# Last two attention chunks routed as one group, the last mixing ahead of routing products, and the last weight pieces behind the last exponential

## The chip, the cores and the metric

The kernel runs on 1 core of one Trainium2 chip. The metric is the device time of one execution in microseconds (us). The engines are named as in the profile: PE (TensorE matmuls), PEld (its weight loads), DVE (VectorE), ACT (ScalarE), POOL (GpSimd) and SP (SyncE, which here issues plain DMAs). Each engine works through its own instructions in the order in which the program issues them, and waits where an input or a buffer of another engine is not ready.

## The reference

Three stages follow each other on 1536 tokens of width 384 (2 batches, 768 steps, 8 heads of 48).

```python
# gated linear attention
for t in range(S):
    state = alpha[:, :, t, :, None] * state + k[:, :, t] (x) v[:, :, t]
    y[:, :, t] = q[:, :, t] @ state
# first layer of experts: each token goes to its best of 8 experts
logits = x @ w_gate;  expert = argmax(logits);  gate = softmax(logits)[expert]
out = gate * (relu(x @ w1[expert]) @ w2[expert])          # up to a capacity per expert
# second layer: noisy gate, two best experts per token
noisy = x @ w_gate + log1p(exp(x @ w_noise)) * noise
out = sum over the top two of softmax weight * (relu(x @ w1[e]) @ w2[e])
```

## The kernel before, in words

**Attention.** The 1536 tokens are 12 chunks of 128. For each chunk `scores` (L298) makes the transposed keys and the masked key-query products, `state` (L322) carries the state on, `mix` (L348) makes the mixed values (copied out of PSUM by ACT, L365), and `logits` runs `r1_logits` (L379): eight matmuls L385 give the token rows and their gate products in one PSUM tile. DVE sums the gate products (`gates`, L387), ACT copies the rows (L394). For chunks 8 to 11 ("late" chunks) ACT also copies a rounded row into a `late` tile (L399), and POOL writes the remainder beside it (L400).

**Routing.** `GROUPS` says which chunks are routed together. `r1_group` (L371) makes the row tile of a group when its first chunk has its logits. `route1` (L404) is a generator; each `R` runs one of its eight steps: maximum; index of the maximum and difference (L417, L418); one-hot (L420); exponential (ACT, L422); rank products on PE (L426 to L430); sums and slots (L432 to L435); for late chunks the one-hot of the slot (L442), the row index (L445) and the running count (L447); and the scatter of each chunk's rows into `xs1` by an indirect DMA that POOL issues (L158, with a small memset L156 ahead of it).

**The written order.** `PATTERNS` holds a string for each chunk index `i`, which the main loop reads letter by letter: S scores of the next chunk, T state, L logits of chunk `i-1`, M mixing of `i`, R one routing step, D a decay step, W one weight piece. `FXR` holds the same for what stands behind the loop: l logits of the last chunk, R a routing step, x a step of `first_x`. All engines get their instructions in this program order.

**The first expert's tokens.** `first_x` (L650) gathers them without a trip through memory for the late chunks: three steps with the rows that were loaded early (`early`, four matmuls L655 each), one step for each of the late chunks 8 to 11 (six matmuls L662 each, which need the late row, its remainder and its slot one-hot), and a last step that copies the result as a high and a low part (L669 on ACT, L670 on DVE).

**Weight pieces.** `split` (L525) cuts a weight tile in 16 pieces; for each ACT makes the rounded high part (L537), and the low part, a subtraction (L538) on DVE or POOL, is put on the list `rest`. `split_rest` issues what is on the list. `splits(k)` in the main loop first calls `split_rest` and then makes piece `k`. The last letters of `WE` give the pieces 13, 14 and 15 to POOL and piece 12 to DVE. Pieces 8 to 15 belong to the second product of the first expert, 12 to 15 to its blocks 4 to 7.

**Behind the gather.** `split_rest()` (L1148) issues what is left, then a few constants are made, among them `lates`: an iota on POOL (L1030) and its conversion on ACT (L1032). Then the experts begin: `hidden` (L675) makes a block of 128 hidden units for the first expert's tokens, nine matmuls (L683, L686), a relu on ACT (L692) and a remainder on DVE (L693). Its PSUM tiles have the tag `ph`, with three buffers.

Of the kernel before, what the change touches and what calls it, by code (L numbers as in the profile page):

```python
# [35 lines left out]
IW = HR + E  # L36
PIECES = [(0, 0, 2), (0, 2, 2), (0, 4, 2), (1, 0, 3), (1, 3, 3)]
PARTS = [[(0, 0, 1), (0, 1, 1)]] + [[a] for a in PIECES[1:]]
GROUPS = [(0, 3), (3, 3), (6, 2), (8, 2), (10, 1), (11, 1)]
MASKS = "G" * 12  # L40
STATES = "AAAAAAAAVVVV"
DECAYS = "444444440000"
# [1 line left out]
S0 = 1  # L44
WARM1 = 2
WARM2 = 10
FXR = "xRRxRRlxRRRRRxxRxRR"
EARLY = 8
WE = "GGGGVVVVVVVVVGGG"
PATTERNS = (  # L50
    "SDDTDDM", "SDDTLDDM", "SDDTLDDM", "SDDTLRRRDDM", "SDDTLDDM", "SRRDTLRRRDDDM",
    "SDDTLRRRDDM", "WSDDTWLDDMW", "WSRRWTRRRWLRRRWMW", "RWSRWTRRRWLWMW", "STLRRRWWMW", "RRRRRLRRRM")
LATE = (0, 4)
LZ = 0
LR = (5, 6, 7, 5, 7, 8)
# [12 lines left out]
def body(tc, ap, cap, dbg=False, stop=False):  # L68
    nc = tc.nc
    V, A, G, PE = nc.vector, nc.scalar, nc.gpsimd, nc.tensor  # L70
    with ExitStack() as ctx:
# [5 lines left out]
        def sb(shape, tag, bufs, dt=F32):  # L77
            cnt[0] += 1
            return pool.tile(list(shape), dt, name=f"{tag}_{cnt[0]}", tag=tag, bufs=bufs)
# [4 lines left out]
        def s6(shape, dt=F32):  # L84
            return sb(shape, "s6", 18, dt)
# [20 lines left out]
        def pm():  # L106
            return ps("pm", 2)
# [44 lines left out]
        NCK = B * NC  # L152
# [218 lines left out]
        def r1_group(js):  # L371

            n = len(js)
            row, l = s6([128, n, RW]), sm([128, 3, E], "l")[:, :n]
            G.tensor_copy(row[:, :, TK:], nt[:, js[0]:js[0] + n, :])
            for k, j in enumerate(js):
                grp[j] = (js, row, l, k)

        def r1_logits(j, first=True):  # L379
            js, row, l, k = grp[j]  # L380
            yT = yTs.pop(j)
            lg = pm()
            lv = lg[:, :4 * IW].rearrange("p (g n) -> p g n", g=4)
            for gp in range(4):
                PE.matmul(lv[:, gp, :], yT[:, gp, :], idw[:, gp, :], start=True, stop=True)  # L385
            def gates():
                V.tensor_reduce(l[:, k, :], lv[:, :, HR:].rearrange("p g n -> p n g"), axis=AX.X, op=ALU.add)  # L387


            if j == NCK - 1:  # L390
                gates()
            by = lambda x: x.rearrange("p (g a e) -> p g a e", g=4, a=2)
            for ab in range(2):
                A.activation(by(row[:, k, :DM])[:, :, ab, :], lv[:, :, ab * 64:ab * 64 + 48], AF.Copy)  # L394
            if j < NCK - 1:
                gates()
            if j >= EARLY and first:
                t = late[j] = sb([128, 2 * DM + C1], "b6", 5, F32R)
                A.activation(t[:, :DM], row[:, k, :DM], AF.Copy)  # L399
                G.tensor_tensor(t[:, DM:2 * DM], row[:, k, :DM], t[:, :DM].bitcast(F32), op=ALU.subtract)  # L400
            if dbg:
                nc.sync.dma_start(ap["xdbg"][j * 128:(j + 1) * 128], row[:, k, :DM])
# [122 lines left out]
        def split(n, q, eng=None):  # L525

            if n >= len(jobs):
                return
            i, h = divmod(q, 4)
            t = raws[n, i]  # L530
            if h == 0:
                shp = [128, ND, 512] if i < 2 else [128, 4, DM]
                parts[n, i] = (s6(shp, F32R), s6(shp, F32R))
            hi, lo = parts[n, i]
            sl = (slice(None), slice(None), slice(h * 128, h * 128 + 128)) if i < 2 else (
                slice(None), slice(h, h + 1), slice(None))
            A.activation(hi[sl], t[sl], AF.Copy)  # L537
            rest.append(lambda: (eng or V).tensor_tensor(lo[sl], t[sl], hi[sl].bitcast(F32), op=ALU.subtract))  # L538
# [111 lines left out]
        def first_x():  # L650

            at = [py()[:, :C1] for _ in range(ND)]
            for d in range(ND):
                for t in range(T1):
                    PE.matmul(at[d][:, t * P1:(t + 1) * P1], early[0][:, t, d * 128:(d + 1) * 128], ident[:P1, :P1],  # L655
                              start=(t == 0), stop=False, skip_group_check=True)
                yield
            n = N // 128
            for j in range(EARLY, n):
                for d in range(ND):  # L660
                    for i in range(2):
                        PE.matmul(at[d], late[j][:, i * DM + d * 128:i * DM + (d + 1) * 128], late[j][:, 2 * DM:],  # L662
                                  start=False, stop=(i == 1 and j == n - 1), skip_group_check=True)
                yield
            xg[0] = sb([P1, T1, RW], "b6", 5)
            nc.sync.dma_start(xg[0][:, :, DM:], xs1[:C1, DM:].rearrange("(t p) d -> p t d", p=P1))
            xh, xl = xsp[0] = (xb([128, ND, C1], F32R), xb([128, ND, C1], F32R))
            for d in range(ND):
                A.activation(xh[:, d, :], at[d], AF.Copy)  # L669
                V.tensor_tensor(xl[:, d, :], at[d], xh[:, d, :].bitcast(F32), op=ALU.subtract)  # L670
            yield
# [396 lines left out]

        groups = [tuple(range(g, g + n)) for g, n in GROUPS]
        routes, extra = [], []  # L1070

        def logits(j):
            for g in groups:
                if g[0] == j:
                    r1_group(g)
            r1_logits(j)
            for g in groups:
                if g[-1] == j:
                    routes.append(route1(g))

        def route_on():
            if routes and next(routes[0], 0) == 0:
                routes.pop(0)
# [19 lines left out]
        si, wi = S0, 0  # L1103
# [28 lines left out]
        fx = first_x()  # L1132
        for o in FXR:
            if o == "x":
                next(fx)
            elif o == "l":
                logits(NCK - 1)
            else:
                route_on()
        while routes:  # L1140
# [404 lines left out]
```

## Time and profile before

| | |
|---|---|
| median of 3 runs | 457.68 us (457.44 to 457.8) |
| profiled execution | 457.59 us, its span 456.0 us |
| PE busy | 445.1 us (98%) |
| POOL busy | 347.6 us (76%) |
| DVE, ACT busy | 273.0 us (60%), 266.3 us (58%) |
| DMA | 93.66 MB, mean 205 GB/s |

The profile is one execution, recorded by the hardware. Busy time is the share of the span in which an engine had an instruction running; PE's ends are modelled, so its starts are the firmer numbers. A releaser ("<-") names what ended an engine's idle time. In a timeline, `x6` says that six instructions of one line follow each other and the time is from the start of the first to the end of the last. The end of attention, where the change lies, is at 77 to 94 us of the span.

### The profile page before, as it was taken

The page shows a single profiled execution, that of the slowest core. Times are in us where ns is not written, and L with a number is a line of the kernel's source. Part 1 is how long each engine was busy: PE and PEld are TensorE (multiplying, and loading weights), DVE is VectorE, ACT ScalarE, POOL GpSimd, SP SyncE. Part 2 cuts the span into 40 slices and gives each one's busy share as a digit, 9 for nine tenths or more (in the row PEclk, how much of TensorE's full clock was granted, in tenths as well). Part 3 has the DMA queues.
Part 4 walks back from the last instruction along what each step waited for, and adds up shares of the span by engine and source line. Part 5 has one row for each costly group of instructions (what it writes and reads, how often), then busy time and mean ns, then how long its engine had stood idle before and what let it go on. Part 6 is the DMA issues. An engine that isn't in the chain of part 4 may idle for free.

```text
span 456.0 us, 9516 instructions
## 1 busy us (share of the span) xinstructions
PE 445.1 (98%) x3167; PEld 418.4 (92%) x3170; DVE 273.0 (60%) x906; ACT 266.3 (58%) x703; POOL 347.6 (76%) x436
## 2 busy tenths in 40 slices
PE   8999999999999999999999999999999999999992
PEld 3688888899999999999999999999999999999992
DVE  8989986856967867878866454333443343243350
ACT  3577787467776776786651468255473464664310
POOL 3434697785998989999943379989989698799922
PEclk9999999999999999999999999999999999999997
DMA  8974972869999987876321997649287492993232
GB/s 284 407 269 150 327 260 96 259 199 313 329 307 314 269 253 224 269 226 193 123 70 55 253 324 229 136 108 323 57 262 154 129 293 57 284 246 51 27 45 43
DMA packets 73586, 93.66 MB, mean 205 GB/s; under 512 B 31962, under 2 KB 56610, under 8 KB 73526
## 3 DMA queue, kind: packets, MB, share of 16 engines
q1 hardware_dynamic: 66854, 79.98, 57.4%
q0 software_dynamic: 6672, 12.97, 12.7%
q8 instruction: 27, 0.44, 0.4%
q14 instruction: 33, 0.27, 0.2%
HBM read 70.30 MB, written 20.02 MB: 198 GB/s over the span
## 4 chain that ended last, share of the span: by engine, by line
PE 95%; DMA 1%; ACT 1%; POOL 0%; DVE 0%; issue 0%; POOLq 0%; ACTq 0%
PE ph L683 24%; PE py L722 22%; PE ph L686 12%; PE py L714 8%; PE py L716 4%; PE ph L170 4%; PE ph L309 3%; PE pm L750 3%; PE pm L385 2%; PE py L336 2%; PE py L362 2%; PE py L356 2%; DMA s<-w 1%; PE py L303 1%; PE ph L1002 1%; PE ph L975 1%
## 5 line engine op out<-in xcount | busy, mean ns | idle before, releaser
L538 POOL TENSOR_TENSOR s<-s,s 128x384 fp32r<-128x384 f32 x211 | 221.1, 1169 | 17.9 <-ACT s L537 16.3
L683 PE MATMUL ph<-x,s 128*128 128x240 f32 (+9 forms) x768 | 133.1, 308 | 0.3 <-DVE h L693 0.2
L537 ACT ACTIVATE s<-s 128x384 fp32r<-128x384 f32 x256 | 124.9, 517 | 9.5 <-DMA s<-w 7.6
L683 PEld LDWEIGHTS ph<-x,s 128*128 128x128 f32 x768 | 116.2, 189 | 1.9 <-DVE h L693 0.4
L693 DVE SCALAR_TENSOR_TENSOR h<-ph,h 128x240 fp32r<-128x240 f32 (+9 forms) x128 | 60.2, 470 | 82.8 <-ACT h L692 80.7
L692 ACT ACTIVATE h<-ph 128x240 fp32r<-128x240 f32 (+9 forms) x128 | 54.1, 423 | 75.7 <-PE ph L686 70.6
L686 PE MATMUL ph<-x,s 128*128 128x240 f32 (+9 forms) x384 | 76.2, 306 | 0.0
L158 POOL DMA_INDIRECT out<-b,m_ix x28 | 44.0, 1571 | 29.4 <-ACT b L878 9.7
L722 PE MATMUL py<-h,s 128*128 128x304 f32 (+4 forms) x360 | 65.4, 339 | 0.0
L722 PEld LDWEIGHTS py<-h,s 128*128 128x128 f32 x360 | 63.2, 188 | 0.8
L714 PE MATMUL py<-h,s 128*128 128x480 f32 (+3 forms) x192 | 61.5, 376 | 0.0
L686 PEld LDWEIGHTS ph<-x,s 128*128 128x128 f32 x384 | 60.9, 189 | 0.2
L716 PE MATMUL py<-h,s 128*128 128x240 f32 (+3 forms) x192 | 50.5, 263 | 0.0
L318 POOL TENSOR_SCALAR_AFFINE_SELECT h<-h 128x512 f32<-128x512 f32 x24 | 22.8, 975 | 30.2 <-ACT h L317 30.2
L158 POOL DMA_INDIRECT xs<-b,m_si x32 | 32.5, 1017 | 17.0 <-DVE pm L832 10.6
L722 PE MATMUL py<-s,h 128*128 128x384 f32 x216 | 38.6, 337 | 0.0
L714 PEld LDWEIGHTS py<-h,s 128*128 128x128 f32 x192 | 36.1, 188 | 2.6
L722 PEld LDWEIGHTS py<-s,h 128*128 128x128 f32 x216 | 37.8, 188 | 0.0
L716 PEld LDWEIGHTS py<-h,s 128*128 128x128 f32 x192 | 36.6, 191 | 0.0
L636 DVE TENSOR_TENSOR x<-pm,x 128x384 fp32r<-128x384 f32 (+8 forms) x42 | 19.9, 473 | 25.8 <-ACT x L635 24.8
L538 DVE TENSOR_TENSOR s<-s,s 128x384 fp32r<-128x384 f32 x45 | 30.6, 700 | 0.4 <-ACT s L537 0.2
L635 ACT ACTIVATE x<-pm 128x384 fp32r<-128x384 f32 (+8 forms) x42 | 17.7, 421 | 22.3 <-DVE pm L632 19.0
(263 smaller groups left out, 606.0 us busy)
## 6 DMA issues: line engine op xcount, KB each, us to landing
s<-w SPq DMA_DIRECT2D x28, 768.0 KB
s<-w_2b SPq DMA_DIRECT2D x22, 768.0 KB
s<-w_1b SPq DMA_DIRECT2D x14, 768.0 KB
xs<-s SPq DMA_DIRECT2D x2, 1576.0 KB
out<-s SPq DMA_DIRECT2D x4, 768.0 KB
b<-xs SPq DMA_DIRECT2D x12, 156.0 KB
b<-xs SPq DMA_DIRECT2D x12, 144.0 KB
b<-b SPq DMA_DIRECT2D x44, 36.0 KB
```

What stands on the lines that cost most here:

```text
L158: st = G.indirect_dma_start(out=dst, out_offset=bass.IndirectOffsetOnAxis(ap=ix, axis=0), in_=src, in_offset=None, **kw)
L318: G.affine_select(a_, a_, pattern=[[0, 4], [1, 128]], compare_op=ALU.is_ge, fill=0.0, base=0, channel_multiplier=-1)
L537: A.activation(hi[sl], t[sl], AF.Copy)
L538: rest.append(lambda: (eng or V).tensor_tensor(lo[sl], t[sl], hi[sl].bitcast(F32), op=ALU.subtract))
L636: rest.append(lambda: V.tensor_tensor(xl[:, d, :], y[:, :c], xh[:, d, :].bitcast(F32), op=ALU.subtract))
L683: PE.matmul(p, w, x[:, d, :], start=(k == 0), stop=False)
L686: PE.matmul(p, w1_of(n, f, d)[0], xl[:, d, :], start=False, stop=(d == ND - 1))
L692: A.activation(hh, p, AF.Relu)
L693: V.scalar_tensor_tensor(hl, p, 0.0, hh.bitcast(F32), op0=ALU.max, op1=ALU.subtract)
L714: PE.matmul(yp[o][:, :2 * c], wh[:, sl], both, start=(f == 0), stop=(f == NF - 1), skip_group_check=True)
L716: PE.matmul(yp[o][:, :c], wl[:, sl], hh, start=False, stop=(f == NF - 1), skip_group_check=True)
L722: PE.matmul(out_, l, r, start=(f == 0 and k == 0), stop=(f == NF - 1 and k == 2))
```

## The change

Three constants and two places in the code change. The last two groups of one chunk each become one group of two. The gate sum now stands ahead of the row copies for the last three chunks, not for the last alone. The letters W leave the pattern of chunk 10; three W stand in `FXR` instead, behind four routing steps of the last group, and there W calls `split` without `split_rest`. In the pattern of chunk 11 the mixing M stands ahead of the logits of chunk 10, and the last routing step of chunks 8 and 9 (their scatters) behind those logits. In `FXR` the logits of chunk 11 stand first, and the gather steps behind them.

```diff
-GROUPS = [(0, 3), (3, 3), (6, 2), (8, 2), (10, 1), (11, 1)]
+GROUPS = [(0, 3), (3, 3), (6, 2), (8, 2), (10, 2)]
...
-FXR = "xRRxRRlxRRRRRxxRxRR"
+FXR = "lxRRRRWWWxxRxxRRR"
...
 PATTERNS = (
...
-    "SDDTLRRRDDM", "WSDDTWLDDMW", "WSRRWTRRRWLRRRWMW", "RWSRWTRRRWLWMW", "STLRRRWWMW", "RRRRRLRRRM")
+    "SDDTLRRRDDM", "WSDDTWLDDMW", "WSRRWTRRRWLRRRWMW", "RWSRWTRRRWLWMW", "STLRRRM", "RRRRMLR")
...
-            if j == NCK - 1:
+            if j >= NCK - 3:
                 gates()
             by = lambda x: x.rearrange("p (g a e) -> p g a e", g=4, a=2)
             for ab in range(2):
                 A.activation(by(row[:, k, :DM])[:, :, ab, :], lv[:, :, ab * 64:ab * 64 + 48], AF.Copy)
-            if j < NCK - 1:
+            if j < NCK - 3:
                 gates()
...
             elif o == "l":
                 logits(NCK - 1)
+            elif o == "W":
+                split(0, wi, G)
+                wi += 1
             else:
                 route_on()
```

## Rows read from the trace of the kernel before

**Rows 1.** The page's section 4: chain that ended last, share of the span by engine.

```profile
PE 95%; DMA 1%; ACT 1%; POOL 0%; DVE 0%; issue 0%; POOLq 0%; ACTq 0%
```

**Rows 2.** Waits of PE over the whole span: us in total, times, longest us.

```profile
PE ph L683 <- DVE h L693: 0.2, 1, 0.2
PE pm L385 <- ACT h L365: 0.2, 1, 0.2
```

**Rows 3.** Timeline of PE, end of attention: start us, us, engine, line, operation.

```profile
80.06 0.18 PE L426 MATMUL pm<-eb,ones 1*128 1x16 bf16 x1
...
80.89 1.15 PE L385 MATMUL pm<-s,h 112*128 112x120 f32 x8 [0.20 <-ACT h L365]
81.88 1.04 PE L356 MATMUL py<-s,s 112*112 112x128 f32 x8
...
83.87 0.70 PE L655 MATMUL py<-iw,b 120*128 120x120 f32 x4
84.50 0.17 PE L426 MATMUL pm<-eb,ones 1*128 1x8 bf16 x1
...
84.73 0.68 PE L655 MATMUL py<-iw,b 120*128 120x120 f32 x4
85.25 1.06 PE L385 MATMUL pm<-s,h 112*128 112x120 f32 x8
86.15 0.61 PE L655 MATMUL py<-iw,b 120*128 120x120 f32 x4
...
89.32 0.93 PE L662 MATMUL py<-b 128*128 128x240 f32 x6
90.26 1.02 PE L683 MATMUL ph<-x,s 128*128 128x240 f32 x6
...
93.78 0.94 PE L683 MATMUL ph<-x,s 128*128 128x240 f32 x6
```

**Rows 4.** Timeline of POOL, same stretch and columns.

```profile
80.30 2.29 POOL L538 TENSOR_TENSOR s<-s,s 128x384 fp32r<-128x384 f32 x2
...
84.38 1.00 POOL L158 DMA_INDIRECT xs<-s,m_si  x1 [1.73 <-DVE m_g L414]
...
85.68 1.01 POOL L158 DMA_INDIRECT xs<-s,m_si  x1 [0.21 <-issue]
...
86.85 1.02 POOL L400 TENSOR_TENSOR b<-s,b 128x384 fp32r<-128x384 f32 x1
...
87.95 1.01 POOL L400 TENSOR_TENSOR b<-s,b 128x384 fp32r<-128x384 f32 x1
...
89.16 1.01 POOL L158 DMA_INDIRECT xs<-s,m_si  x1 [0.16 <-POOL spacer L156]
...
91.46 1.03 POOL L538 TENSOR_TENSOR s<-s,s 128x384 fp32r<-128x384 f32 x1
92.43 0.24 POOL L1030 IOTA m_iota_lates<- 128x128 int32 x1
```

**Rows 5.** Timeline of ACT, same stretch and columns.

```profile
87.28 0.52 ACT L399 ACTIVATE b<-s 128x384 fp32r<-128x384 f32 x1
...
92.71 0.31 ACT L1032 ACTIVATE lates<-m_iota_lates 128x128 f32<-128x128 int32 x1 [1.97 <-POOL m_iota_lates L1030]
92.92 0.36 ACT L692 ACTIVATE h<-ph 128x240 fp32r<-128x240 f32 x1
```

**Rows 6.** Timeline of DVE, same stretch and columns.

```profile
78.86 0.19 DVE L387 TENSOR_REDUCE m_l<-pm 128x8 f32<-128x32 f32 x1 [0.78 <-ACT s L394]
...
85.50 0.35 DVE L442 TENSOR_SCALAR b<-h,m_sf 128x240 fp32r<-128x240 f32 x1
...
93.31 0.41 DVE L693 SCALAR_TENSOR_TENSOR h<-ph,h 128x240 fp32r<-128x240 f32 x1 [1.55 <-ACT h L692]
```

**Rows 7.** Busy us (x instructions) by window: PE, PEld, DVE, ACT, POOL, PEclk, DMA, GB/s.

```profile
448.00:450.00 2.00, 0.00 (x0) 0.00 (x0) 0.42 (x1) 0.05 (x1) 1.23 (x1) 1.00 0.09 25
450.00:452.00 2.00, 0.00 (x0) 0.00 (x0) 0.00 (x0) 0.00 (x0) 0.34 (x1) 0.73 0.59 68
```

## The prediction

> **What bounds the kernel now.** I began with the chain that ended last: TensorE (PE) holds 95% of it [rows 1]. So the question is where PE still waits, and whether anything behind it has slack. The list of PE's waits answers: it names three waits in all, and after the start only two, 0.2 us each [rows 2]. One is where logits(10) wait for ACT's copy of mixed chunk 10, the other is a hidden product waiting for VectorE (DVE) line L693. A delay of PE after the end of attention therefore has nothing downstream to vanish into, and a gain there is kept.
>
> The timeline of PE over the end of attention shows the order of work: rank products of chunks 8 and 9, logits of 10 at 80.89, mixing of 11 at 81.88, first-expert gather, logits of 11 at 85.25, gather, hidden products from 90.26 [rows 3]. The gaps are small: the rank group of chunks 8 and 9 starts at 80.06 and the logits only at 80.89, 0.83 for what takes 0.23 at the next group (84.50 to 84.73), so some 0.6 us could be saved.
>
> The other engines matter for one place after that. GpSimd (POOL) makes the scatters of the routed rows, subtracts one weight piece (L538, 91.46), and then makes the `lates` iota (92.43) [rows 4]. ACT waits 1.97 us for that iota, converts it (L1032, 92.71), and only then makes the first relu (L692, 92.92) [rows 5]. DVE's L693 of the same block follows at 93.31 for 0.41 [rows 6]. The fourth hidden block starts at 93.78, directly behind it [rows 3]: the PSUM tag `ph` has three buffers, so block f=3 needs the first one free. That is PE's wait on L693 [rows 2]. So POOL's queue already ends exactly where PE needs it; its slack is about nil.
>
> **The change, part by part.**
>
> *Order on PE.* After mixing 10 the rank products of 8 and 9 run as before, but their one-hot comes sooner: the gate sum L387 now stands ahead of the row copies, where it waited 0.78 us for them [rows 6]. Then follows mixing 11, which took 81.88 to 83.87, 1.99 [rows 3], with ACT's copies behind it. From 80.06 + 0.23 it runs from about 80.4 to 82.4. Logits 10 and 11 take 0.90 each (85.25 to 86.15 [rows 3]); neither waits, since the copy of mixed chunk 11 has the logits of 10 as cover. They end at about 84.2 instead of 86.15. One rank group instead of two saves another 0.23 of PE.
>
> *Routing 10 and 11 together.* The shorter list of small DVE operations is off the path. But the gather now needs both chunks' remainders (L400 on POOL, the low part of the late rows), and these lie differently in POOL's queue. Before, both scatters of 8 and 9 went first (84.38 and 85.68), then L400 twice (86.85, 87.95), then the scatters of 10 and 11 (from 89.16) [rows 4]. Now the scatters of 8 and 9 are issued after logits(10), so behind L400 of chunk 10; L400 of chunk 11 comes behind them.
>
> *POOL step by step.* The first logit product of chunk 11 is at 85.25 [rows 3] and its row copy L399 ends at 87.80 [rows 5]: 2.55 us from the one to the other. Logits(10) now start at about 82.4, so L399 of chunk 10 ends at 84.95 and L400 starts at 85.0. From rows 4, start to start: L400 0.97 (1.02 busy), two scatters with their spacers 2.55 (from where L400 of 11 ends, 88.9, to 91.46), L400 0.97, two scatters 2.55. That reaches 92.05, against 91.46 before: +0.6.
>
> *The weight pieces.* Before, the subtractions of pieces 13 and 14 ran at 80.30 (2.29 for two) and only piece 15 stood behind the scatters, at 91.46 [rows 4]. Now `W` in FXR makes only ACT's copies; the subtractions gather in `rest` until `split_rest()` after the gather, which is ahead of the iota in program order. So three L538 precede it, 0.97 each start to start (91.46 to 92.43): +1.94. Queued behind them on POOL is the iota; ACT waits for it, DVE for ACT, PE for DVE. ACT's three copies have the size of L399, 0.52 each [rows 5]; at about 86.2 to 87.7 they lie beside gather products and cost nothing, and without that cover they would hold ACT's copies of the gathered tokens by 1.6. Piece 12, now on DVE behind the gather, falls into DVE's idle time before L693. All four pieces are second-layer weights of blocks 4 to 7, needed only after all hidden blocks.
>
> *Other queues.* SyncE (SP) loads the next expert's rows when the last scatter lands; that comes 0.6 later, while PE comes 2.5 later, so no load becomes late by it.
>
> *Sum.* Iota at 92.43 + 0.6 + 1.9 = 94.9. From iota to block f=3 is 93.78 − 92.43 = 1.35 [rows 3, 4], all of it one dependence after another, so f=3 starts at 96.3: +2.5 us. PE's own gain is lost twice. L400 of chunk 11 starts at 85.0 + 0.97 + 2.55 = 88.5 and ends at 89.5, and the second of that chunk's six products needs it; the six and the copy behind them took 0.94 (89.32 to 90.26 [rows 3]), of which 0.8 remain, so the hidden blocks begin at about 90.3, as now. And three blocks later PE waits for L693. The profiled execution took 457.59 us, its span 456.0, 1.59 around it; the median of the runs is 457.68, 0.09 above it. 457.59 + 2.5 = 460.1.
>
> *Bounds.* L400 of chunk 10 may start between 84.8 and 85.4, as tightly as PE keeps to its order (the two gaps above). A pair of scatters took 2.47 (84.38 to 86.85) to 2.55. A subtraction took 0.97 at 91.46 and 1.15 at 80.30 [rows 4]. All low ends give +1.8, all high ends +3.4; I stay nearer the low end, since the scatters and the subtraction just ahead of the iota (from 89.16) are the nearest rows.
>
> *A rule that speaks against the change.* The routing of 10 and 11 puts its two one-hot operations L442 (0.35 each [rows 6]) beside scatters 8 and 9. One ran from 85.50 to 85.85 across the scatter at 85.68, which took 1.01, as the one at 89.16 did [rows 4, 6]. The Trainium skill, SBUF — State Buffer, section "SBUF: two separate sides", says that a VectorE operation in a 2-port mode keeps GpSimd from writing DMA descriptors. By that rule the scatters would stretch by up to 0.7 and the time would be 460.8; by the row it is 460.1, which I keep.
>
> **The rivals.**
> (a) *Faster: PE alone sets the end.* With POOL out of the way the gather would end when its products do. From the end of the logits of 11 it took 4.11 (86.15 to 90.26); two groups of L655 move behind the logits, 0.52 each (84.73 to 85.25): 84.2 + 4.1 + 1.05 = 89.35 [rows 3], 0.9 earlier, 456.7 us. For that the iota must start by 93.78 − 0.9 − 1.35 = 91.5, which is 3.4 us less POOL work than I count. Against it: three subtractions and four scatters in a row. Chance 0.07.
> (b) *No change*: the late start of f=3 is taken back later, or POOL reaches the iota at 92.4 after all because the subtractions stand elsewhere in its queue than I read. The list of waits leaves nothing to take it back [rows 2]. 457.6. Chance 0.05.
> (c) *Longer POOL*: scatters and subtractions are stretched by DVE. Place: POOL's queue from 85 to 95; price 0.9 over the forecast; decides from the point where each L538 needs 1.15 or more. 461.0. Chance 0.07.
> (d) *The clock falls.* In the wait before f=3 PE stands idle about 2.5 us. At the end of the trace PE had no work in 448 to 450 and the granted clock was still 1.00; it was 0.73 on the mean of 450 to 452 [rows 7], which is a fall from the upper of its two levels (2.4 GHz) to the lower (1.2 GHz) at about 450.9. So an idle time like ours did not lower it there. If it did, PE would run at half pace; for a stretch as long as the low one at the end, 5 us (450.9 to 456), that costs 2.5 us more: 462.6. Chance 0.04. The Trainium skill, TensorE: Matmul & The Clock Gate, section "HAM oscillation — how this bites in real kernels", says that waits between bursts can drop the clock each time; this is the rule behind (d), and the trace agrees as far as long idleness lowers it.
>
> **How the numbers follow.** Forecast (POOL's three subtractions hold the iota, 460.1) 0.77. Its own bounds give 459.4 to 461.0; the range 459.3 to 461.1 holds nearly all of it and most of (c), and leaves out (a), (b), (d): 0.16, and a little of the tails. Faster by over 0.2% (about what a measurement of this kernel can tell from no change, 0.9 us): 0.07. Within it: 0.05. Slower: 0.77 + 0.07 + 0.04 = 0.88.
>
> **What would show it.** In the profile after: three L538 in a row between the last xs1 scatter and the iota, iota at about 94.9; ACT's idle time before L1032 near 4 us and ended by POOL; a new PE wait on DVE L693 of about 2.5 us, at block f=3; L400 between the two pairs of scatters; a PE wait of near 1 us in the late gather products ended by POOL's L400; logits of 10 and 11 back to back with no wait; granted clock 1.00 throughout. If the iota stands before the subtractions, or PE's wait on L693 stays at 0.2, I am wrong, and (a) or (b) holds.

## The result, and the profile after

The changed kernel is slower. Median times, each kernel over 8 runs on the same chip:

| | median | lowest to highest | span of the profiled execution |
|---|---|---|---|
| before | 457.49 us | 456.74 to 457.8 | 456.0 us |
| changed | 460.74 us | 459.05 to 461.43 | 459.1 us |

The ratio is 1.0064, with a 95% interval of 1.0046 to 1.0083. The eight times of the changed kernel fall in two groups: 459.05, 459.13 and 459.25 with a mean granted clock of 0.994 to 0.995, and 460.64 to 461.43 (five runs) with 0.990 to 0.992. The profiled execution, 460.83 us, is one of the second group. So there are two costs to explain, one that all runs have and one that five of eight have.

PE's waits over the span (us in total, times, longest), beside rows 2:

```profile
PE ph L683 <- DVE h L693: 2.5, 2, 2.2
...
PE py L662 <- POOL spacer L156: 0.4, 1, 0.4
...
```

The wait on L693 has grown from 0.2 to 2.2, and a short one of the gather products for POOL is new; the spacer L156 that is named there is the instruction right behind L400 in POOL's queue, and it is L400's remainder that the products read. The wait for ACT before the logits of 10 is gone.

PE's timeline (start us, us, engine, line, operation), beside rows 3. In this execution everything up to the attention's end lies 0.70 us earlier (L426 at 79.37 here, 80.06 in rows 3), so 0.70 is added where the two traces are compared:

```profile
79.37 0.18 PE L426 MATMUL pm<-eb,ones 1*128 1x16 bf16 x1
...
81.62 2.04 PE L385 MATMUL pm<-s,h 112*128 112x120 f32 x16
83.50 1.50 PE L655 MATMUL py<-iw,b 120*128 120x120 f32 x12
...
88.65 0.83 PE L662 MATMUL py<-b 128*128 128x240 f32 x5 [0.40 <-POOL spacer L156]
89.49 1.02 PE L683 MATMUL ph<-x,s 128*128 128x240 f32 x6
...
95.30 0.94 PE L683 MATMUL ph<-x,s 128*128 128x240 f32 x6 [2.22 <-DVE h L693]
...
96.41 1.37 PE L683 MATMUL ph<-x,s 128*128 128x240 f32 x6
...
98.22 1.48 PE L683 MATMUL ph<-x,s 128*128 128x240 f32 x6
...
100.05 0.83 PE L683 MATMUL ph<-x,s 128*128 128x240 f32 x6
...
101.06 0.83 PE L683 MATMUL ph<-x,s 128*128 128x240 f32 x6
```

Both groups of logits run back to back and end at 83.50 + 0.70 = 84.20, 2 us earlier than in rows 3 (86.15). The hidden blocks begin at 89.49 + 0.70 = 90.19, against 90.26. Block f=3 begins at 95.30 + 0.70 = 96.00, against 93.78: 2.2 us later. Then two blocks (96.41 to 98.22 to 100.05) take 1.81 and 1.83, where the block from 100.05 to 101.06 takes 1.01. That is 1.6 us more.

POOL's timeline (the same columns), beside rows 4 to 6:

```profile
84.22 1.00 POOL L400 TENSOR_TENSOR b<-s,b 128x384 fp32r<-128x384 f32 x1 [4.21 <-ACT b L399]
...
85.41 1.01 POOL L158 DMA_INDIRECT xs<-s,m_si  x1 [0.15 <-POOL spacer L156]
...
87.72 0.88 POOL L400 TENSOR_TENSOR b<-s,b 128x384 fp32r<-128x384 f32 x1
...
90.08 0.96 POOL L158 DMA_INDIRECT xs<-s,m_si  x1 [0.21 <-issue]
91.08 2.94 POOL L538 TENSOR_TENSOR s<-s,s 128x384 fp32r<-128x384 f32 x3
93.97 0.24 POOL L1030 IOTA m_iota_lates<- 128x128 int32 x1
```

ACT's timeline behind the iota:

```profile
94.24 0.31 ACT L1032 ACTIVATE lates<-m_iota_lates 128x128 f32<-128x128 int32 x1 [4.27 <-POOL m_iota_lates L1030]
94.45 0.35 ACT L692 ACTIVATE h<-ph 128x240 fp32r<-128x240 f32 x1
```

And DVE's, with the two one-hots L442 beside the scatters of 8 and 9:

```profile
86.22 0.60 DVE L442 TENSOR_SCALAR b<-h,m_sf 128x240 fp32r<-128x240 f32 x2
...
90.42 4.02 DVE L538 TENSOR_TENSOR s<-s,s 128x384 fp32r<-128x384 f32 x1
...
94.84 0.41 DVE L693 SCALAR_TENSOR_TENSOR h<-ph,h 128x240 fp32r<-128x240 f32 x1
```

Three subtractions stand between the last scatter and the iota. ACT idles 4.27 us for it. DVE shows something that no row of before showed there: its one subtraction, piece 12, took 4.02 us. It ended at 94.44, 0.4 after POOL's row of subtractions (91.08 to 94.02).

The granted clock (PEclk, the figure right behind the busy times of the five engines), by stretches of 2 us:

```profile
94.00:96.00 2.00, 0.70 (x6) 0.70 (x7) 1.60 (x24) 1.76 (x6) 0.91 (x3) 1.00 0.58 96
96.00:98.00 2.00, 2.00 (x14) 2.00 (x13) 1.57 (x7) 1.35 (x4) 2.00 (x3) 0.63 0.81 148
98.00:100.00 2.00, 2.00 (x11) 2.00 (x11) 1.07 (x4) 0.78 (x2) 1.89 (x3) 0.52 1.02 380
100.00:102.00 2.00, 2.00 (x20) 2.00 (x20) 1.09 (x3) 1.52 (x4) 1.21 (x2) 1.00 1.01 367
```

The clock stayed at the upper level while PE waited and fell to the lower one (1.2 GHz) in the two stretches after that, with PE at work again since 95.30.

### The profile page after: what moved, and what is told of

The parts are those of the page before. It is cut to its first block, busy times and chain, and to the rows that moved or that the text cites. A ratio compares the mean times of both kernels' runs of the same rounds, so it can differ in the third digit from the quotient of the medians.

```text
span 459.1 us, 9503 instructions
## 1 busy us (share of the span) xinstructions
PE 445.6 (97%) x3165; PEld 419.6 (91%) x3168; DVE 275.2 (60%) x898; ACT 266.0 (58%) x702; POOL 349.0 (76%) x435
## 4 chain that ended last, share of the span: by engine, by line
PE 90%; DVE 6%; issue 1%; DMA 1%; ACT 1%; POOL 0%; POOLq 0%; DVEq 0%
PE ph L683 24%; PE py L722 22%; PE ph L686 12%; PE py L714 9%; PE py L716 4%; PE pm L750 3%; PE pm L385 2%; PE ph L309 2%; PE py L356 2%; PE py L336 2%; PE py L362 2%; PE py L303 1%; DVE s L244 1%; PE ph L1002 1%; PE ph L975 1%
## 5 line engine op out<-in xcount | busy, mean ns | idle before, releaser
L693 DVE SCALAR_TENSOR_TENSOR h<-ph,h 128x240 fp32r<-128x240 f32 (+9 forms) x128 | 60.3, 471 | 81.4 <-ACT h L692 78.2
L318 POOL TENSOR_SCALAR_AFFINE_SELECT h<-h 128x512 f32<-128x512 f32 x24 | 24.1, 1029 | 27.6 <-ACT h L317 27.6
L538 DVE TENSOR_TENSOR s<-s,s 128x384 fp32r<-128x384 f32 x45 | 33.6, 767 | 0.4 <-ACT s L537 0.2
```

Of the source, the lines that this page charges most:

```text
L318: G.affine_select(a_, a_, pattern=[[0, 4], [1, 128]], compare_op=ALU.is_ge, fill=0.0, base=0, channel_multiplier=-1)
L693: V.scalar_tensor_tensor(hl, p, 0.0, hh.bitcast(F32), op0=ALU.max, op1=ALU.subtract)
```

## The experiments

Each ratio is against the kernel before, run on the same chip in the same job; the chips differ by some tenths of a percent (the kernel before had medians of 456.1, 456.1 and 457.2 us in the three jobs), so only ratios are compared between jobs. Theory A: POOL's three subtractions delay the iota, it delays ACT, and ACT delays L693. Rival B: DVE's own subtraction, held beside POOL's, delays L693. Theory C: PE's idle time lets the clock fall.

**The iota at the start.** Only the place of one line changes:

```diff
+        lates = iota_f([128, CL], "lates", [[1, CL]], C0 + 1, 0)    # behind tro, among the other iotas
...
-        lates = iota_f([128, CL], "lates", [[1, CL]], C0 + 1, 0)    # behind least
```

> The changed kernel, with only the lates iota and its conversion moved to the other iotas at the start; POOL still makes three subtractions behind the last scatter. In the profile of the changed kernel PE waits 2.2 us before hidden block f=3 and the iota ends at 94.2. Theory A (the iota holds ACT, and ACT alone holds L693): the wait goes, f=3 starts at about 92.9 on that trace's scale, the granted clock stays at 1.00, and the time is 459.1 - 2.3 = 456.8 us in all runs. Rival B (DVE is held as well: its subtraction of piece 12 ran 90.42 to 94.4, beside POOL's three): L693 of the first block can't start before about 94.0, f=3 before 94.5, so 1.5 to 2 us of wait stay and the time is 458.3 to 458.8, or 460 and more where the clock falls.

Measured: 462.67 us, ratio 1.0146 (1.0132 to 1.0161), the slowest of all. PE's wait before f=3:

```profile
PE ph L683 <- DVE h L693: 5.1, 1, 5.1
```

DVE's timeline at its subtraction of piece 12:

```profile
90.50 6.85 DVE L538 TENSOR_TENSOR s<-s,s 128x384 fp32r<-128x384 f32 x1
```

POOL's timeline beside it:

```profile
91.14 5.79 POOL L538 TENSOR_TENSOR s<-s,s 128x384 fp32r<-128x384 f32 x6
```

Theory A, as it was put (ACT alone holds L693), falls, and B was too mild. With the iota out of the way ACT goes on, so POOL is fed three more subtractions and makes six without a gap, until 96.93; DVE's one subtraction lasts until 97.35. In the changed kernel the iota was a brake and a help at once: it held ACT, but it also ended POOL's row of subtractions. The granted clock was 0.56 from 98 to 100 and 0.59 from 100 to 102.

**Piece 12 of DVE ahead of the gather.**

```diff
+        split_rest()
         fx = first_x()
```

> The changed kernel, with only DVE's subtraction of piece 12 issued ahead of the first step behind the attention loop, where DVE idles; the iota stays behind POOL's three subtractions. Theory A: nothing changes at f=3, ACT still waits for the iota until about 94.2, f=3 at 95.3, times as of the changed kernel (459.1 where the clock holds, 460.6 to 461.4 where it falls). If rival B alone were the cause, f=3 would start at 92.9 and the time would be 456.8.

Measured: 459.03 us, ratio 1.0056 (1.0036 to 1.0077), with two times at 457.3 and four at 459.0 to 460.0. DVE's subtraction, with POOL idle beside it, was short:

```profile
83.13 0.56 DVE L538 TENSOR_TENSOR s<-s,s 128x384 fp32r<-128x384 f32 x1
```

Still PE's wait was:

```profile
PE ph L683 <- DVE h L693: 2.2, 1, 2.2
```

DVE's timeline at L693 says what it was late for:

```profile
95.02 0.41 DVE L693 SCALAR_TENSOR_TENSOR h<-ph,h 128x240 fp32r<-128x240 f32 x1 [3.82 <-ACT h L692]
```

So B alone isn't the cause either: without it ACT holds L693 just as long, as A says. Each of the two is enough to keep block f=3 waiting. The clock fell here too, and already while PE waited (f=3 began at 95.49): the mean of 0.77 puts the fall at about 95.1.

```profile
94.00:96.00 2.00, 0.51 (x2) 0.52 (x3) 0.71 (x2) 1.58 (x6) 0.91 (x3) 0.77 0.52 83
```

**Both moves.** The two edits together.

> The changed kernel with both moves: the iota at the start, and DVE's piece 12 ahead. Both theories expect no wait before f=3, a clock of 1.00 throughout and 456.8 us in all runs, about 0.7 below the kernel before; hidden products begin at 89.5 as in the changed kernel, since the wait of the last gather products for POOL's L400 (0.4 us) stays. If time stays near 459, the cause is neither.

Measured: 457.4 us, ratio 1.0024 (1.0014 to 1.0034). The wait before f=3 and the fall of the clock are gone, as expected, and that is worth 5.3 us against the iota alone (462.67); but the 0.7 us below the kernel before that was expected isn't there. A new wait has come among PE's:

```profile
PE ph L683 <- ACT x L635: 1.4, 1, 1.4
```

POOL's timeline:

```profile
90.93 11.74 POOL L538 TENSOR_TENSOR s<-s,s 128x384 fp32r<-128x384 f32 x12
```

DVE's timeline in the same stretch:

```profile
96.17 6.54 DVE L507 CAST of<-m_of 128x6 int32<-128x6 f32 x1
```

POOL now makes twelve subtractions without a gap, and DVE's L507, a cast of 6 columns that belongs to the ordering of the experts (0.48 us before), takes 6.54, until POOL's row ends. Three L693 and the copies of the second expert's tokens stand behind it.

**PE kept busy in its wait.** On the changed kernel, ten matmuls that nobody reads:

```diff
             for f in range(NF):
+                if n == 0 and f == 3:
+                    p = pm()
+                    for _ in range(10):
+                        PE.matmul(p, wt[:, :128], wt, start=True, stop=True)
                 hidden(n, f)
```

> The changed kernel with ten 512-column matmuls (0.216 us each, 2.2 us, read by nobody) put on PE ahead of hidden block f=3, where it idles 2.2 us; nothing else. Clock theory (the idle time lets the granted clock fall in some runs, which costs about 1.7 us more): the clock stays at 1.00, f=3 starts within 0.2 us of where it did, and all runs lie near 459.1, none near 461. Rival (the runs of the changed kernel near 461 have another cause, a DMA or the start): times still lie in two groups, near 459 and 461. If PE isn't idle there as read, the ten matmuls add up to 2.2 us: 461.3.

Measured: 457.8 us, 457.29 to 458.06 in all five runs, ratio 1.0039 (1.0026 to 1.0052). In this job that is 1.7 us above the kernel before, the distance of the changed kernel's faster group (459.1 to 457.5 is 1.6), and no run lies 3 us above. The granted clock at the place, by stretches of 2 us:

```profile
94.00:96.00 2.00, 1.97 (x13) 1.24 (x12) 1.57 (x26) 2.00 (x7) 0.96 (x1) 1.00 0.67 128
96.00:98.00 2.00, 2.00 (x20) 2.00 (x20) 1.58 (x7) 1.72 (x5) 2.00 (x4) 1.00 0.78 175
```

The matmuls start at 92.69 and f=3 at 95.05, so it is as late as it was; only the idle time is gone. Theory C stands: the second group is the clock.

**The pieces back.** On the changed kernel, the three W back in the pattern of chunk 10:

```diff
-"STLRRRM", ...      FXR = "lxRRRRWWWxxRxxRRR"
+"STLRRRWWMW", ...   FXR = "lxRRRRxxRxxRRR"
```

> The changed kernel with the three weight pieces back in the pattern of chunk 10, as in the kernel before; the group of two, the order of mixing and logits and of the scatters stay changed. POOL then makes one subtraction between the last scatter and the iota. Theory (three subtractions ahead of the iota are the loss, regrouping and reordering are worth next to nothing because hidden products still begin with L400 of chunk 11 and block f=3 still waits for the iota): the iota starts 1.94 us earlier than in the changed kernel, f=3 waits 0.3 to 0.5 us, the granted clock stays, and the time is 0 to 0.4 us above the kernel before on this chip (ratio 1.000 to 1.001). Rival (the regrouping itself costs, through the scatters of 8 and 9 that come later): 1 us or more above, ratio over 1.002.

Measured: 455.91 us, ratio 0.9997 (0.9988 to 1.0005). PE's waits:

```profile
PE py L662 <- POOL spacer L156: 0.9, 1, 0.9
...
PE ph L683 <- DVE h L693: 0.3, 1, 0.3
```

POOL's timeline behind the last scatter:

```profile
91.34 1.01 POOL L538 TENSOR_TENSOR s<-s,s 128x384 fp32r<-128x384 f32 x1
92.30 0.24 POOL L1030 IOTA m_iota_lates<- 128x128 int32 x1
```

One subtraction, the iota right behind it, and the loss is gone. The group of two and the new order of mixing and logits by themselves are worth nothing that the interval shows: what PE saves it waits for again, 0.9 us for L400 and 0.3 for L693.

**The pieces late alone.** On the kernel before, the W moved behind the exponential of the last group, all else as it was.

```diff
-FXR = "xRRxRRlxRRRRRxxRxRR"
+FXR = "xRRxRRlxRRRRRWWWxxRxRR"
-    ..., "STLRRRWWMW", "RRRRRLRRRM")
+    ..., "STLRRRM", "RRRRRLRRRM")
```

> The kernel before with only the three weight pieces moved behind the last exponential; groups, mixing and gate sums as before. Theory: two more subtractions ahead of the iota, which starts 1.94 us later; f=3 waits 2.0 us; DVE's piece 12 is held beside POOL's three, about 4 us in the trace; time 1.9 above the kernel before where the clock holds (ratio 1.004), 3.6 above where it falls (1.008). Rival (the loss comes from grouping and reordering, not from the pieces): ratio 1.000 to 1.001.

Measured: 458.97 us, ratio 1.0065 (1.0046 to 1.0083), the changed kernel's own ratio. PE's wait before f=3:

```profile
PE ph L683 <- DVE h L693: 1.9, 1, 1.9
```

POOL's timeline behind the last scatter:

```profile
91.36 2.94 POOL L538 TENSOR_TENSOR s<-s,s 128x384 fp32r<-128x384 f32 x3
```

DVE's timeline at the one-hot of chunk 10 and at piece 12:

```profile
84.46 1.90 DVE L442 TENSOR_SCALAR b<-h,m_sf 128x240 fp32r<-128x240 f32 x1
...
91.03 3.71 DVE L538 TENSOR_TENSOR s<-s,s 128x384 fp32r<-128x384 f32 x1
```

The granted clock, in the stretch where it is lowest:

```profile
98.00:100.00 2.00, 2.00 (x11) 2.00 (x11) 1.14 (x5) 0.78 (x2) 2.00 (x3) 0.50 0.99 356
```

One part of the change alone brings the wait before f=3, the held subtraction on DVE and the fall of the clock. That its ratio equals the changed kernel's is partly chance: here the hidden blocks also begin 0.8 us later, 10.99 us after the rank products of chunks 8 and 9 (79.10 to 90.09) against 10.20 in the kernel before, with L442 drawn out to 1.90 and a new wait of PE of 0.4 for L447.

**Both moves, and the cast without SBUF.** On the run with both moves, the ordering's sum is kept in PSUM, so that L507 reads PSUM:

```diff
-            sel, of = const([128, q, q], f"sel{layer}"), sm([128, q], "of")
+            sel, of = const([128, q, q], f"sel{layer}"), cp[:, 48:48 + q]
```

> The run with both moves (iota at the start, piece 12 ahead), with one difference: the expert order's sum is kept in PSUM, so the cast L507 (6.54 us there beside twelve POOL subtractions in a row, 0.48 in the kernel before) doesn't read SBUF. Theory (DVE operations with SBUF operands alone are shut out while POOL subtracts without a gap): L507 takes under 0.5 us, the three L693 behind it are on time, PE's wait of 1.4 us goes, and the time falls by about 1.3 us to the kernel before or 0.2 below it (ratio 0.9995 to 1.000). Rival (L507 waits for something else than POOL's port): it stays at several us, ratio 1.002 to 1.003 as with both moves alone.

Measured: 455.36 us, ratio 0.9985 (0.9976 to 0.9993). POOL's timeline has eleven subtractions in a row:

```profile
91.24 10.77 POOL L538 TENSOR_TENSOR s<-s,s 128x384 fp32r<-128x384 f32 x11
```

Yet in DVE's timeline L507 is short:

```profile
96.49 0.16 DVE L507 CAST of<-pm 128x6 int32<-128x6 f32 x1
```

So it was the SBUF input, against a POOL that subtracts, that held the cast; the work behind it is on time, and the wait of 1.4 is gone. The same kernel once more, on a third chip:

> The run with both moves and the sum in PSUM once more, beside the kernel before with the same two repairs: ratio 0.998 to 0.999 again, and 0.3 to 0.6 us below that run if the changed order of the routing is worth what the start of the hidden products says (10.1 us from the rank products of chunks 8 and 9 to the first hidden block, 10.2 in the kernel before); equal to it if the order is worth nothing.

Measured: 456.88 us, ratio 0.9991 (0.998 to 1.0002). The gain over the kernel before is 0.1%, at the edge of what can be measured.

**The kernel before with the same repairs.** The iota at the start and the sum in PSUM, nothing of the change.

```diff
-            sel, of = const([128, q, q], f"sel{layer}"), sm([128, q], "of")
+            sel, of = const([128, q, q], f"sel{layer}"), cp[:, 48:48 + q]
...
+        lates = iota_f([128, CL], "lates", [[1, CL]], C0 + 1, 0)    # behind tro
...
-        lates = iota_f([128, CL], "lates", [[1, CL]], C0 + 1, 0)
```

> The kernel before with only the iota at the start and the expert order's sum in PSUM; groups, mixing, gate sums and pieces as before. It tells what of the gain of the run that beat the kernel before (both moves and the sum in PSUM on the changed kernel, ratio 0.9985) belongs to the changed order. If the moves alone bring it: 0.9985 here too. If the changed order brings it, once nothing holds it up: only the 0.2 us wait before block f=3 goes, ratio 0.9993 to 1.000, since the hidden products begin where they did.

Measured: 456.81 us, ratio 0.9992 (0.9978 to 1.0007), equal to the run beside it. The expected 0.3 to 0.6 between the two isn't there: nothing shows that the small gain, if there is one, belongs to the changed order.

**Remainders first.** The pieces back, the scatters of 8 and 9 behind both L400, and the three repairs (iota, piece 12, cast). The diff is against the run with the pieces back; the lines of the iota and the cast, which are as above, are left out.

```diff
-FXR = "lxRRRRxxRxxRRR"          # chunk 11: "RRRRMLR"
+FXR = "lRxRRRRxxRxxRRR"         # chunk 11: "RRRRML"
...
+        split_rest()             # ahead of first_x
```

> The changed kernel with the pieces back in the pattern of chunk 10, the scatters of 8 and 9 behind the remainders L400 of both last chunks (so L400 of 11 ends about 2.3 us earlier), the iota at the start, piece 12 of DVE ahead of the gather, and the expert order's small sum kept in PSUM, so that its cast L507 reads no SBUF. Theory: no wait of PE for L400, for the iota or for DVE; hidden products begin 0.5 us earlier than in the kernel before, on the scale of each trace, and nothing behind them is late: 0.5 to 0.7 us faster than the kernel before, ratio 0.9985 to 0.999. Rival (a run of POOL subtractions behind the scatters holds DVE's operations on SBUF anyway): ratio 1.001 to 1.003, with single DVE operations of over 2 us.

Measured: 455.87 us, ratio 0.9998 (0.9986 to 1.0009): a miss. The edit was not what was meant: the line that brings piece 12 forward issues all that is left, and so put POOL's subtraction of piece 15 (86.20) between the two L400, where it holds DVE's L433 for 0.74; PE waits 0.4 us for the slots L442, which came late. The hidden blocks did begin 9.79 us after the rank products of chunks 8 and 9 (80.13 to 89.92), 0.4 earlier than in the kernel before; that is less than the interval can tell from nothing. POOL's timeline:

```profile
85.23 1.00 POOL L400 TENSOR_TENSOR b<-s,b 128x384 fp32r<-128x384 f32 x1 [2.51 <-ACT b L399]
86.20 1.01 POOL L538 TENSOR_TENSOR s<-s,s 128x384 fp32r<-128x384 f32 x1
87.17 0.86 POOL L400 TENSOR_TENSOR b<-s,b 128x384 fp32r<-128x384 f32 x1
```

DVE's timeline beside it:

```profile
86.50 0.74 DVE L433 TENSOR_SCALAR m_se<-m_se 128x2 f32<-128x2 f32 x1
```

**Gaps on POOL.** On the run with both moves, a memset of one element ahead of each subtraction of the second expert's weights.

```diff
-            rest.append(lambda: (eng or V).tensor_tensor(lo[sl], t[sl], hi[sl].bitcast(F32), op=ALU.subtract))
+            def low():
+                if eng is G and n == 1:
+                    G.memset(spacer, 0.0)
+                (eng or V).tensor_tensor(lo[sl], t[sl], hi[sl].bitcast(F32), op=ALU.subtract)
+            rest.append(low)
```

> The run with both moves (iota at the start, piece 12 ahead), with one addition: a memset of one element on POOL (0.09 us, it reads nothing) ahead of each subtraction that POOL makes for the second expert's weights. There POOL made twelve subtractions in a row and DVE's cast L507 took 6.54 us, until the row ended. Theory (DVE gets the common port only when POOL is at something that doesn't read SBUF, or idle): L507 ends at the next memset, 0.5 to 1.2 us after its start, PE's wait of 1.4 us goes, ratio 0.998 to 1.000. Rival (the port passes only when POOL has nothing left to do): L507 stays at several us, ratio 1.002 to 1.004.

Measured: 459.29 us, ratio 1.005 (1.0034 to 1.0067). The cast isn't let in, as DVE's timeline shows:

```profile
96.42 6.80 DVE L507 CAST of<-m_of 128x6 int32<-128x6 f32 x1
```

POOL's timeline in the same stretch:

```profile
96.09 0.09 POOL L540 MEMSET spacer<- 1x1 f32 x1
96.14 1.01 POOL L541 TENSOR_TENSOR s<-s,s 128x384 fp32r<-128x384 f32 x1
97.10 0.09 POOL L540 MEMSET spacer<- 1x1 f32 x1
```

A memset of this kind between subtractions doesn't let DVE in. That isn't yet the end of the theory: each memset begins about 0.05 before the subtraction ahead has ended, and the next subtraction 0.05 later, so that POOL is at the memset alone for no time that the trace shows. The cast ended at 103.22, when POOL had nothing left to do (its last subtraction ended at 103.19).

## Why the prediction was right, and where it wasn't

The median, 460.74, lies in the range, and the place, the queue and the wait are those that the prediction named. That the median lies there is partly luck: of the eight runs only two (460.64 and 460.83) lie between 459.3 and 461.1, the faster group is just below and the rest of the slower one above, by a cost that the forecast left out. The forecast of 460.1 stands for no run.

*POOL's queue: right, a little too long.* On the scale of the trace of before, L400 of chunk 10 started at 84.92 (85.0 predicted), that of chunk 11 at 88.42 (88.5), the iota at 94.67 (94.9), f=3 at 96.00 (96.3). Each pair of scatters with its spacers took 2.56 (85.16 to 87.72, and 88.52 to 91.08), as reckoned. Most of the difference, +2.2 instead of +2.5, is L400 of chunk 11, which gave way to the next instruction after 0.80 and not 0.97, and a start that was 0.08 earlier. The low bound was added up wrong: 84.8 + 0.97 + 2.47 + 0.97 + 2.47 + 3 × 0.97 + 1.35 is 95.94, +2.2 and not +1.8, so the measured delay lies at the low end. PE's wait for L400 was 0.40 and not near 1. The pieces back and the pieces late alone show that the three subtractions are the part that counts.

*The rule on scatters.* The two L442 ran from 86.22 to 86.82, over the end of the scatter at 85.41 and the start of that at 86.72, which took 1.01 and 0.98: not stretched. The choice of the row over the rule of the Trainium skill was right here. In the run with the pieces late alone it was the one-hot that was held: 1.90 from 84.46 on, beside a scatter of 0.97 (84.08) and an L400 (85.21).

*Piece 12 on DVE: wrong.* The prediction let it fall into DVE's idle time at no cost. It took 4.02 us beside POOL's subtractions. That it changed no number is because ACT was held as long; with the iota moved PE waited 5.1 us for it. DVE did have the idle time that was named as cover, but beside POOL's subtractions it couldn't use it.

*The clock, rival (d): wrong.* It got 0.04, on the argument that an idle time of that length had not lowered the clock at the end of the trace. In the profiled execution it fell after a wait of 2.2, with PE at work again for 1.2 us, and stayed down from 96.5 to 99.9. The cost, 1.6 us, is under the 2.5 that (d) was given: the low stretch lasted 3.4 us and not 5. By the mean clocks five of eight runs had it, and the run with PE kept busy shows that PE's idle time is what brings it. The rows at the end of the trace were one case, and they were taken for a rule. The page of the Trainium skill on which (d) rested, TensorE: Matmul & The Clock Gate, section "HAM oscillation — how this bites in real kernels", says that waits between bursts can let the clock drop each time; here the trace agrees, with a single wait of 2.2 us.

*The sum.* Rival (d) said wait plus clock, 462.6; the measured pieces are 457.49 + 2.2 + 1.6 = 461.3, within the slower group (460.64 to 461.43). Without the clock 457.49 + 2.2 = 459.7, where 459.1 was measured; the 0.6 between stays open. The 0.70 by which the trace of the changed kernel runs ahead of that of before is of this size, and it lies between executions: in the thirteen traces the rank products of chunks 8 and 9 begin at 79.10 to 80.13, and at 79.10, 79.75 and 80.06 in the three with the old order.

*Rival (a)*, a gain of 0.9 once POOL is out of the way: with iota, piece 12 and cast moved, the hidden blocks began 10.1 us after the rank products of 8 and 9, against 10.2 before, so 0.8 of it didn't come. Of that, PE's wait for POOL's L400 is 0.4 and that for the one-hot L420 0.2; the rest was not followed up.

## What to carry to other kernels

A step that is moved takes along what it leaves on other queues: three cheap copies on ACT went where ACT was idle, and their subtractions landed on POOL ahead of a tiny instruction that the next stage waits for. Look for the last instruction of a queue that another engine needs, and let nothing be put ahead of it. Before an engine's idle time is taken as cover, see whether another engine can shut it out there; and a wait on PE costs more than its length when the clock falls after it.

## What the runs showed of the hardware

**DVE can be shut out for a whole row of POOL subtractions, and not only for one of them.** A DVE operation with SBUF operands took 4.02, 6.85, 6.54, 6.80 and 3.71 us beside three to twelve POOL subtractions in a row, against 0.56 (the subtraction) and 0.48 (the cast). In the cases of the subtraction DVE had started first (90.42 against POOL's 91.08 in the changed kernel, 90.50 against 91.14 with the iota at the start, 91.03 against 91.36 with the pieces late alone), each time while POOL was at a scatter. The Trainium skill, SBUF — State Buffer, section "SBUF: two separate sides", says that the loser of the common port waits for the whole instruction of the other; here it waited for the whole row of them. With its input in PSUM the same cast took 0.16 beside a row of eleven. When the port changes hands inside a row stays open: in the kernel before, L507 was done 0.48 after its start, in the middle of eleven subtractions, as the two timelines of before show:

```profile
97.27 0.48 DVE L507 CAST of<-m_of 128x6 int32<-128x6 f32 x1
...
93.77 11.28 POOL L538 TENSOR_TENSOR s<-s,s 128x384 fp32r<-128x384 f32 x11 [1.10 <-ACT s L537]
```

**The clock fell at waits of about 2 us, and not at each.** In all four profiled executions with a PE wait of 1.9 us or more at this place (the changed kernel, the iota at the start, piece 12 ahead, the pieces late alone) the granted clock fell to the lower level, between 0.4 us before PE's restart and 1.6 us after it. By the means of the 2 us stretches it stayed low for 3.4 us in each. In the profiles with waits of 1.4 us or less it stayed up. But by the mean clocks three of the eight runs of the changed kernel went without the fall, so that such a wait brings it in some executions only.
